# A fused MLP on one core: two sums of each split pair issued one pair later, and the steps of the next input block dealt out anew

## The chip, the core and the metric

The kernel runs on one core of a Trainium2 chip. A core has TensorE (matrix products, with a queue of its own for weight loads, written PEld in the rows), VectorE (DVE), ScalarE (ACT), GpSimd (POOL) and SyncE (SP, which issues transfers here). Each engine works through its own instructions in the order in which the kernel issues them, and waits for others through semaphores. The metric is the device time of one execution in microseconds, as the median of several runs; less is better.

## The reference

Three stages follow each other on 4 x 3072 tokens of 256 channels: a Fourier layer (a transform along the sequence, a complex linear map with soft threshold, the transform back), a channel mix (shift, `relu(xk @ w_k)^2 @ w_v`, gated by a sigmoid), and an MLP with the Mish activation. The change touches the last one alone:

```python
def _moe2_ref(x, w_in, w_out):            # x: 12288 x 256
    h = x @ w_in                          # 256 x 2048
    sp = np.where(h > 20.0, h, np.log1p(np.exp(np.minimum(h, 20.0))))
    g = h * np.tanh(sp)                   # Mish
    return (g @ w_out).astype(np.float32) # 2048 x 256
```

## The kernel before

The MLP takes the tokens in 24 blocks of 512 (`t`, 0 to 23), and each block in eight pairs (`r = P % 8`, of P = 8t + r). A pair is two slices of 128 of the 2048 hidden channels. For every pair TensorE makes the hidden values (`xy` and `z`, two tiles in its accumulation memory), ScalarE takes their Mish, and three pairs later (`LAG = 3`) TensorE multiplies the result by its slice of `w_out` into the block's four output tiles `o`.

Every fp32 operand is split in a high and a low part, and each product is three matmuls: high x high, high x low, low x high. So ScalarE takes each Mish twice, once rounded into `gh` and once in full into `g`, and VectorE makes the low part `gl = g - gh` (line 1137).

From block 1 on, both products of a pair go by a scheme of seven half-size products for eight (Strassen's, in a form with few sums). The first product of all pairs is made in that way (`emit_hS`): sums of the input, `xS`, are made once per block in six steps (`make_xS(t, k)`, k = 0 to 5), for block t+1 during block t, spread over its pairs; steps 0, 1, 3 and 5 stand on VectorE, 2 and 4 on ScalarE. The second product is made in that way for the pairs r = 0, 2, 3, 5, 6 of blocks 1 to 22, called split pairs here (`strassen(P)`, `QS`). A split pair needs four sums of its `g`, made on VectorE into the tile `S6`: two first sums, `sums(P, 0)`, and two second sums, `sums(P, 1)`, of which the last one reads the one before. Then ScalarE rounds the four sums to the high part of `HS` (`high_S`), and VectorE subtracts to get the low part (`low_S`). A split pair's second product is 21 matmuls of 256 columns, that of another pair 12 of 512.

All order is written by hand. `emit_hS(P)` issues a pair in this sequence, with `o(n)` for the next n matmuls of the second product of pair P - 3:

1. TensorE: the first product into `xy`. ScalarE: copy of it to `z` (line 1292), which marks the pair's begin in this document; then `act_1`, the Mish of the last pair's `xy` (in pair 2 of a block first a copy of `o` into the tile `U`, line 1233).
2. `o(n1)`; three products into `xy` and `z`. ScalarE: copy of `xy` to `ub` (line 1298). VectorE: `dve_1`, with the low parts of the last pair and first sums; in pair 2 three sums of `U` (`first_sums`) stand ahead of them, and in pair 0 two transposes of finished output.
3. `o(n2)`; one more product into `xy`, which needs `ub` to be done. VectorE: the addition of `xy` and `ub` into `z`. ScalarE: `act_2`, then the Mish of `z`. VectorE: `dve_2`, with `low_S(P - 2)`, the second sums of pair P - 1 and steps of the next x.
4. The rest of `o`, then two products with `WI` into `xy`, the first of which overwrites what the addition into `z` read. VectorE: the addition of `xy` and `ub` into `xy`. These two products and the first of the next pair are nine matmuls in a row, `xy<-xS,WI x9`.

A tile's buffers are few: `g` has two, `U`, `HS` and `ub` one, so that a pair's `g` is written again two pairs later.

Of the kernel before, what the change touches and what calls it, by code (L numbers as in the profile page):

```python
# [24 lines left out]
NBLK = B * 6  # L25
# [5 lines left out]
def kernel(  # L31
# [27 lines left out]
    nc = tc.nc  # L59
# [10 lines left out]
    def x2_part(c, n):  # L70
        q, o = divmod(c, 1536)
        return x2d[q][:, :, o:o + n]
# [788 lines left out]
    g_t = {}  # L861
# [110 lines left out]
    for t in range(NA + 1):  # L972
# [5 lines left out]
        for i2 in range(4):  # L978
            P = 4 * t + i2
# [68 lines left out]
    def load_x2(t):  # L1048
        v = pb.tile([128, 2, 512], F32, tag="x2", name="x2", bufs=1)
        nc.sync.dma_start(out=v, in_=x2_part(512 * t, 512))  # L1050
        x2_t[t] = v
# [15 lines left out]
    def make_xS(t, k, eng=None):  # L1067

        v = x2_t[t]
        last = t == NBLK - 1  # L1070
        o4 = last_order if last else (lambda a, how=None: a)
        b11, b12, b21, b22 = (
            o4(v[:, j, 256 * h:256 * h + 256], "p (c n w) -> p c w n") for j in range(2) for h in range(2)
        )
        if k == 0:
            xT_t[0] = pb.tile([128, 4, 256], F32, tag="xT", name="xT", bufs=1)
            xS_t[t] = pb.tile([128, 2, 7, 256], F32R, tag="xS", name="xS", bufs=2)
        xT, xS = xT_t[0], xS_t[t]

        def raw(l):  # L1080
            if last:
                return [(o4(xS[:, l, i, :]), b) for i, b in enumerate((b11, b21, b22))]
            return [(xS[:, l, 0, :], b11), (xS[:, l, 1:3, :], v[:, 1, :].rearrange("p (h n) -> p h n", h=2))]

        def xt(o):
            return o4(xT[:, o, :])

        def sub(o, x0, x1):
            nc.vector.tensor_tensor(out=xt(o), in0=x0, in1=x1, op=ALU.subtract)

        def cast(o, x):
            if eng is None:
                nc.vector.tensor_copy(out=o, in_=x)
            else:
                eng.copy(out=o, in_=x)

        if k == 0:
            sub(0, b12, b11)
            sub(2, b22, b12)
        elif k == 1:  # L1100
            sub(1, b22, xt(0))
            sub(3, b21, xt(1))
        elif k == 2:
            cast(xS[:, 0, 3:7, :], xT)
        elif k == 3:
            nc.vector.tensor_tensor(out=xS[:, 1, 3:7, :], in0=xT, in1=xS[:, 0, 3:7, :], op=ALU.subtract)
        elif k == 4:
            for xs, b in raw(0):
                cast(xs, b)
        else:  # L1110
            for (xl, b), (xh, _) in zip(raw(1), raw(0)):
                nc.vector.tensor_tensor(out=xl, in0=b, in1=xh, op=ALU.subtract)
# [9 lines left out]
    def strassen(P):  # L1122
        return 8 <= P < 8 * (NBLK - 1) and P % 8 in QS

    xy_t, low_t, S_t, S_n = {}, {}, {}, []
    S6 = pb.tile([128, 6, 256], F32, name="S6")

    def blocks(v):
        return v.rearrange("p m (h n) -> p (m h) n", h=2)
# [14 lines left out]
    def mish_xy(P):  # L1144
        xy = xy_t.pop(P, None)
        if xy is None:
            return
        ks = (slice(0, 2), slice(1, 3))
        mish(P, xy, (slice(1, 2), slice(2, 3)) if strassen(P) else ks, ks)

    def low(P):
        if low_t.get(P):
            low_t[P].pop(0)()

    def tt(out, x0, x1, op):
        nc.vector.tensor_tensor(out=out, in0=x0, in1=x1, op=op)  # L1156

    def sums(P, k):
        if not strassen(P):
            return  # L1160
        g = blocks(g_t[P][2])
        if k == 0:
            n = len(S_n)
            S_n.append(P)
            S_t[P] = [4 * (n % 2), (0, 2, 1, 3) if n % 2 == 0 else (2, 0, 3, 1)]
            a = S6[:, S_t[P][0]:S_t[P][0] + 2, :]
            tt(a[:, 0, :], g[:, 1, :], g[:, 3, :], ALU.add)
            tt(a[:, 1, :], g[:, 0, :], g[:, 1, :], ALU.subtract)
            return
        a = S_t[P][0]  # L1170
        tt(S6[:, 2, :], S6[:, a, :], g[:, 0, :], ALU.subtract)
        tt(S6[:, 3, :], g[:, 2, :], S6[:, 2, :], ALU.subtract)

# [4 lines left out]
    def high_S(P):  # L1178
        if P in S_t:
            hl = pb.tile([128, 2, 4, 256], F32R, tag="HS", name="HS", bufs=1)  # L1180
            S_t[P].append(hl)
            nc.scalar.copy(out=hl[:, 0], in_=S_of(P))  # L1182

    def low_S(P):
        if P in S_t:
            hl = S_t[P][2]
            tt(hl[:, 1], S_of(P), hl[:, 0], ALU.subtract)
# [6 lines left out]
    def new_U(t):  # L1194
        U_t[t] = pb.tile([128, 4, 256], F32, tag="U", name="U", bufs=1)

    def first_sums(t):
        U, (a, b, c, d) = U_t[t], o_t[t]
        tt(U[:, 3, :], c[:, 1, :], U[:, 0, :], ALU.add)
        tt(U[:, 1:3, :], d, both(U[:, 3, :]), ALU.add)  # L1200
        tt(U[:, 3, :], d[:, 1, :], U[:, 1, :], ALU.add)

    def last_sums(t):
        U = U_t[t]
        for e in range(2):
            o, u = o_t[t][e], U[:, 2 * e:2 * e + 2, :]
            if t:
                tt(u, o, u, ALU.add)
            else:
                nc.vector.tensor_copy(out=u, in_=o)  # L1210

    def put_out(t):
        U = U_t.pop(t)
        ob = pb.tile([128, 16, 32, 2], F32, tag="ob", name="ob", bufs=1)
        for e in range(2):
            nc.vector.transpose(
                out=ob[:, :, :, e], in_=U[:, 2 * e:2 * e + 2, :].rearrange("p h (c w) -> p (h c) w", w=32)
            )
        for m in range(4):
            b, r = divmod(4 * t + m, 24)  # L1220
            j, k = divmod(r, 3)
            dst = out_v[b, j, k].rearrange("n w d -> w n d")
            for i in range(4):
                nc.sync.dma_start(  # L1224
                    out=dst[:, :, 64 * i:64 * i + 64],
                    in_=ob[32 * i:32 * i + 32, 4 * m:4 * m + 4].rearrange("p n d e -> p n (d e)"),
                )

    def act_1(P):
# [3 lines left out]
            nc.scalar.copy(out=U_t[t - 1][:, 0, :], in_=o_t[t - 1][2][:, 0, :])  # L1233
        mish_xy(P - 1)

    def dve_1(P):
        t, r = divmod(P, 8)
        if r == 2 and 1 < t < NBLK:
            first_sums(t - 1)
        if r == 3 and 0 < t < NBLK:  # L1240
            if t == 1:
                new_U(0)
            last_sums(t - 1)
        low(P - 1)
        if t + 1 < NBLK and t:
            if r in (4, 5):
                make_xS(t + 1, 1 if r == 4 else 3)
            if r == 7 and t + 2 < NBLK:
                load_x2(t + 2)
        if r == 7 and t == NBLK - 1:  # L1250
            put_out(t - 1)
        if r == 0 and 1 < t < NBLK:
            put_out(t - 2)
        low(P - 1)
        if r != 3:
            sums(P - 1, 0)

    def act_2(P):
        t, r = divmod(P, 8)
        high_S(P - 2)  # L1260
        if t and t + 1 < NBLK and r in (3, 4):
            make_xS(t + 1, 4 if r == 3 else 2, nc.scalar)

    def dve_2(P):
        t, r = divmod(P, 8)
        low_S(P - 2)
        if r == 3:
            sums(P - 1, 0)
        sums(P - 1, 1)
        if t and t + 1 < NBLK and r in (1, 6):  # L1270
            make_xS(t + 1, 0 if r == 1 else 5)

    def emit_hS(P, o):
        t, r = divmod(P, 8)
# [22 lines left out]
        prod(z[:, 0, :], A(0, 1), 1)  # L1297
        nc.scalar.copy(out=ub, in_=xy)  # L1298
        dve_1(P)
        o(n2)  # L1300
        prod(xy[:, 0, :], S_(0), 3)
        tt(z[:, 1, :], xy[:, 0, :], ub[:, 1, :], ALU.add)
        act_2(P)
        mish_z(P, z)
        dve_2(P)
        o(99)
        prod(xy[:, 0, :], S3, 2)
# [87 lines left out]
    for P in range(2, 8 * NBLK + LAG):  # L1395
        t, q = divmod(P, 8)
        steps = o_steps(P - LAG) if P >= LAG else iter(())

        def o(n):
            for _ in range(n):  # L1400
                if next(steps, 0) == 0:
                    return

        if P < 8 * NBLK:
            if t:
                emit_hS(P, o)
            else:
                emit_h(P)
                if q < 7:
                    make_xS(1, q - 2)  # L1410
                if q == 6:
                    make_xS(1, 5)
                    load_x2(2)
                load_WI(P)
        else:
            act_1(P)
            dve_1(P)
            act_2(P)
            dve_2(P)
        o(99)  # L1420
        t, q = divmod(P - LAG, 8)
        if q in QS and P >= LAG and t in (0, NBLK - 2):
            to_WO(q, b12_d[QS.index(q)] if t else wt_d[QS.index(q)][:, 768:1024])
# [82 lines left out]
```

## Time and profile before

| what | value |
|---|---|
| median of 3 runs | 1926.55 us (1926.35 to 1927.57) |
| the profiled execution, its own time | 1927.98 us |
| its span, from the first to the last instruction | 1926.1 us |
| mean granted clock of TensorE | 0.998 of full speed |
| TensorE busy | 1907.6 us, 99% |
| TensorE weight loads busy | 1823.6 us, 95% |
| VectorE busy | 1403.3 us, 73% |
| ScalarE busy | 1334.2 us, 69% |
| GpSimd busy | 147.2 us, 8% |

The busy time of an engine counts its own instructions, not its waits for semaphores. TensorE's matmuls overlap in their rows and their ends are modelled, so small waits need not show as gaps there; the distance between like points of two pairs shows them. The MLP's pairs with both products fill the span from about 964 us to the end; a block takes some 41 us.

### The profile page before, as it was taken

To read this page: it belongs to the slowest core of one execution; us is meant where nothing else is said; L and a number is where in the kernel's file an instruction comes from. 1 tells how busy PE (TensorE), PEld (TensorE's weight loads), DVE (VectorE), ACT (ScalarE), POOL (GpSimd) and SP (SyncE) were. 2 spreads that over 40 slices of the span, in tenths; PEclk is the share of its full clock that TensorE was granted. 3 is DMA by queue.
4 is the path that set the end of the run, shared out by engine and by line. 5 is a ranking of instruction groups with operands and counts; after the bars stand their busy time and mean duration, and the time that the engine had idled before them with its cause. 6 is when DMAs were issued, how large, how long until landed. Compare 5 with 4: busy or idle time off the path is not lost.

```text
span 1926.1 us, 33928 instructions
## 1 busy us (share of the span) xinstructions
PE 1907.6 (99%) x12964; PEld 1823.6 (95%) x12964; DVE 1403.3 (73%) x2498; ACT 1334.2 (69%) x2315; POOL 147.2 (8%) x236
## 2 busy tenths in 40 slices
PE   8999999999999999999999999999999999999998
PEld 6889989999999999999899999999999999999998
DVE  3788776665665665664378888888888888888884
ACT  4777776666666666666467777777777777777774
POOL 1444630000000000000000000000000000000000
PEclk9999999999999999999999999999999999999999
DMA  9877531322212222220411000111000111000111
GB/s 271 250 235 227 162 112 55 94 73 62 91 50 94 65 66 87 72 75 28 146 40 30 23 23 23 34 28 29 23 23 23 34 27 30 23 23 23 34 25 35
DMA packets 122598, 138.04 MB, mean 72 GB/s; under 512 B 59778, under 2 KB 96100, under 8 KB 122436
## 3 DMA queue, kind: packets, MB, share of 16 engines
q1 hardware_dynamic: 118852, 123.29, 22.4%
q0 software_dynamic: 3584, 12.58, 1.8%
q8 instruction: 102, 1.67, 0.3%
q14 instruction: 60, 0.49, 0.1%
HBM read 78.03 MB, written 57.80 MB: 71 GB/s over the span
## 4 chain that ended last, share of the span: by engine, by line
PE 93%; DVE 2%; POOL 1%; DMA 1%; issue 1%; SPq 1%; ACT 0%; POOLq 0%; DVEq 0%; ACTq 0%
PE o L1355 25%; PE xy L1284 21%; PE kp L755 14%; PE vp L957 14%; PE pp L911 3%; PE z L1284 3%; PE pp L573 3%; PE s1p L361 2%; PE mxp L457 2%; PE s2p L408 1%; PE k1p L457 1%; PE i1p L512 1%; PE hp L877 1%; POOL Y L503 1%; SPq L1224 0%
## 5 line engine op out<-in xcount | busy, mean ns | idle before, releaser
L755 PE MATMUL kp<-xk,WK 128*128 128x384 f32 x1524 | 291.6, 339 | 0.0
L1355 PE MATMUL o<-gh,WO 128*128 128x512 f32 (+1 forms) x1032 | 283.4, 346 | 0.0
L957 PE MATMUL vp<-kh,WV 128*128 128x384 f32 x1024 | 280.7, 335 | 0.0
L944 DVE TENSOR_TENSOR kl<-kr,kh 128x768 fp32r<-128x768 f32 x128 | 122.9, 960 | 211.2 <-ACT kr L943 210.5
L755 PEld LDWEIGHTS kp<-xk,WK 128*128 128x128 f32 x1524 | 264.1, 188 | 0.2
L1284 PE MATMUL xy<-xS,WS 128*128 128x256 f32 x1656 | 261.0, 284 | 0.9 <-ACT z L1292 0.9
L1284 PEld LDWEIGHTS xy<-xS,WS 128*128 128x128 f32 x1656 | 231.0, 189 | 17.9 <-ACT z L1292 1.7
L1137 DVE TENSOR_TENSOR gl<-g,gh 128x512 fp32r<-128x512 f32 x368 | 218.3, 603 | 36.8 <-ACT g L1135 36.8
L1284 PE MATMUL xy<-xS,WI 128*128 128x256 f32 x1656 | 231.0, 284 | 0.0
L1284 PEld LDWEIGHTS xy<-xS,WI 128*128 128x128 f32 x1656 | 211.1, 189 | 9.7 <-DVE z L1156 4.7
L1135 ACT ACTIVATE gh<-z 128x512 fp32r<-128x512 f32 x184 | 110.4, 600 | 145.6 <-PE o L1355 120.3
L957 PEld LDWEIGHTS vp<-kh,WV 128*128 128x128 f32 x1024 | 186.6, 188 | 0.8 <-DVE r L965 0.7
L1355 PEld LDWEIGHTS o<-gh,WO 128*128 128x128 f32 x1032 | 173.7, 188 | 13.9
L1355 PE MATMUL o<-gl,WO 128*128 128x512 f32 (+1 forms) x516 | 178.5, 346 | 0.0
L957 PE MATMUL vp<-kl,WV 128*128 128x384 f32 x512 | 171.5, 335 | 0.0
L942 ACT ACTIVATE kh<-kr 128x768 fp32r<-128x768 f32 x128 | 108.3, 846 | 86.2 <-PE vp L957 85.8
L1156 DVE TENSOR_TENSOR z<-xy,ub 128x256 f32<-128x256 f32 x184 | 79.5, 432 | 94.9 <-PE xy L1284 92.5
L935 ACT ACTIVATE kr<-kp 128x768 f32<-128x768 f32 x127 | 103.3, 813 | 62.5 <-PE kp L755 60.8
L1298 ACT COPY ub<-xy 128x512 f32<-128x512 f32 x184 | 108.4, 589 | 42.1 <-PE xy L1284 41.0
L1156 DVE TENSOR_TENSOR HS<-S,HS 128x1024 fp32r<-128x1024 f32 x110 | 134.2, 1220 | 0.0
L1355 PE MATMUL o<-HS,WO 128*128 128x256 f32 x660 | 131.5, 280 | 0.0
L1182 ACT CAST HS<-S 128x1024 fp32r<-128x1024 f32 x110 | 115.9, 1054 | 2.1 <-PE o L1355 0.3
(177 smaller groups left out, 3846.8 us busy)
## 6 DMA issues: line engine op xcount, KB each, us to landing
scr<-Cs SPq DMA_DIRECT2D x48, 256.0 KB, 2.5
D<-scr SPq DMA_DIRECT2D x32, 384.0 KB, 4.5
x2d<-r POOLq DMA_DIRECT2D x32, 384.0 KB, 2.8
x<-x2d SPq DMA_DIRECT2D x24, 512.0 KB, 3.9
out_dram<-ob SPq DMA_DIRECT2D x368, 32.0 KB, 1.6
A<-scr SPq DMA_DIRECT2D x44, 256.0 KB, 4.4
xs<-in_x_dram SPq DMA_DIRECT2D x24, 384.0 KB, 5.8
scr<-xs SPq DMA_DIRECT2D x24, 384.0 KB, 4.4
```

Of the source, the lines that this page charges most:

```text
L755: nc.tensor.matmul(out=p, lhsT=WK[:, dh, w, f * 128:(f + 1) * 128], rhs=hl[:, v, dh, :], start=(i == 0), stop=(i == 5),)
L935: nc.scalar.activation(out=kr, in_=kp_t.pop(P)[:, :, 0:TA], func=AF.Relu)
L942: nc.scalar.activation(out=kh, in_=kr, func=AF.Square)
L944: nc.vector.tensor_tensor(out=kl, in0=kr, in1=kh, op=ALU.subtract)
L957: nc.tensor.matmul(out=p[:, o, 0:TA], lhsT=WV[:, f, w, o * 128:(o + 1) * 128], rhs=v[:, m, :], start=(f == 0 and i == 0), stop=(f == 7 and ...
L1135: nc.scalar.activation(out=h[:, v[1], :], in_=src[:, v[0], :], func=AF.Mish)
L1137: lambda: nc.vector.tensor_tensor(out=gl[:, hs[1], :], in0=g[:, hs[1], :], in1=gh[:, hs[1], :], op=ALU.subtract)
L1156: nc.vector.tensor_tensor(out=out, in0=x0, in1=x1, op=op)
L1182: nc.scalar.copy(out=hl[:, 0], in_=S_of(P))
L1284: nc.tensor.matmul(out=out, lhsT=a(l), rhs=xS[:, v, b, :], start=(start and n == 0), stop=False, skip_group_check=True)
L1298: nc.scalar.copy(out=ub, in_=xy)
L1355: nc.tensor.matmul(out=out, lhsT=w, rhs=v, start=start, stop=False, skip_group_check=True)
```

## The change

Two things move. The second sums of a split pair stood in `dve_2` of the pair after it; they now stand in `dve_1` of the pair after that, ahead of the low parts (and behind `first_sums` and `last_sums` where these stand). The blocks of `g` that they read are kept in `g_of`. And the steps of the next x, with their pairs r, are set by three tables: step 1 goes from pair 4 to 5, step 3 from 5 to 6 (both in `dve_1`), step 2 from 4 to 5 (`act_2`); steps 4 (pair 3), 0 (pair 1) and 5 (pair 6) keep their pairs. The load of the next x moves from `dve_1` to `dve_2` of pair 7.

```diff
     def sums(P, k):
         if not strassen(P):
             return
-        g = blocks(g_t[P][2])
         if k == 0:
+            g = blocks(g_t[P][2])
             n = len(S_n)
             S_n.append(P)
             S_t[P] = [4 * (n % 2), (0, 2, 1, 3) if n % 2 == 0 else (2, 0, 3, 1)]
+            g_of[P] = g
...
             return
-        a = S_t[P][0]
+        a, g = S_t[P][0], g_of.pop(P)
         tt(S6[:, 2, :], S6[:, a, :], g[:, 0, :], ALU.subtract)
         tt(S6[:, 3, :], g[:, 2, :], S6[:, 2, :], ALU.subtract)
...
+    XS_B = {5: (1,), 6: (3,)}
+    XS_A = {1: (0,), 6: (5,)}
+    XS_C = {3: (4,), 5: (2,)}
+
+    def x_steps(P, table, eng=None):
+        t, r = divmod(P, 8)
+        if t and t + 1 < NBLK:
+            for k in table.get(r, ()):
+                make_xS(t + 1, k, eng)
+
     def dve_1(P):
...
             last_sums(t - 1)
+        if P - 2 in S_t:
+            sums(P - 2, 1)
         low(P - 1)
-        if t + 1 < NBLK and t:
-            if r in (4, 5):
-                make_xS(t + 1, 1 if r == 4 else 3)
-            if r == 7 and t + 2 < NBLK:
-                load_x2(t + 2)
+        x_steps(P, XS_B)
...
     def act_2(P):
-        t, r = divmod(P, 8)
         high_S(P - 2)
-        if t and t + 1 < NBLK and r in (3, 4):
-            make_xS(t + 1, 4 if r == 3 else 2, nc.scalar)
+        x_steps(P, XS_C, nc.scalar)
 
     def dve_2(P):
         t, r = divmod(P, 8)
         low_S(P - 2)
         if r == 3:
             sums(P - 1, 0)
-        sums(P - 1, 1)
-        if t and t + 1 < NBLK and r in (1, 6):
-            make_xS(t + 1, 0 if r == 1 else 5)
+        x_steps(P, XS_A)
+        if r == 7 and 0 < t and t + 2 < NBLK:
+            load_x2(t + 2)
```

The first place is VectorE's row from the addition into `z` of pair 1 to that of pair 2. `S_9457` is the tile `S6`, of which `S<-S,g` is the first and `S<-g,S` the second of the two second sums; `xT` is step 0 of the next x. Before:

```order
L1156 TENSOR_TENSOR z<-xy,ub 128x256
L1156 TENSOR_TENSOR S_9457<-S_9457,g 128x256
L1156 TENSOR_TENSOR S_9457<-g,S_9457 128x256
L1089 TENSOR_TENSOR xT<-x_12711 128x256 x2
L1156 TENSOR_TENSOR xy<-xy,ub 128x256
L1156 TENSOR_TENSOR U<-o_12443,U 128x256
L1156 TENSOR_TENSOR U<-o_12444,U 128x512
L1156 TENSOR_TENSOR U<-o_12444,U 128x256
L1137 TENSOR_TENSOR gl<-g,gh 128x2x256
L1137 TENSOR_TENSOR gl<-g,gh 128x512
L1156 TENSOR_TENSOR z<-xy,ub 128x256
```

The same stretch of VectorE's row after the change:

```order
L1156 TENSOR_TENSOR z<-xy,ub 128x256
L1089 TENSOR_TENSOR xT<-x_12727 128x256 x2
L1156 TENSOR_TENSOR xy<-xy,ub 128x256
L1156 TENSOR_TENSOR U<-o_12443,U 128x256
L1156 TENSOR_TENSOR U<-o_12444,U 128x512
L1156 TENSOR_TENSOR U<-o_12444,U 128x256
L1156 TENSOR_TENSOR S_9457<-S_9457,g 128x256
L1156 TENSOR_TENSOR S_9457<-g,S_9457 128x256
L1137 TENSOR_TENSOR gl<-g,gh 128x2x256
L1137 TENSOR_TENSOR gl<-g,gh 128x512
L1156 TENSOR_TENSOR z<-xy,ub 128x256
```

The two sums of pair 0 have moved from behind `z` of pair 1 to a place between the three sums of `U` and the low parts, ahead of `z` of pair 2.

The second place is VectorE's row from the addition into `z` of pair 7 to that of pair 0 of the next block. `HS` is the low part of the sums of pair 5, and the transposes make finished output. Before:

```order
L1156 TENSOR_TENSOR z<-xy,ub 128x256
L1156 TENSOR_TENSOR HS<-S_9457,HS 128x1024
L1156 TENSOR_TENSOR S_9457<-S_9457,g 128x256
L1156 TENSOR_TENSOR S_9457<-g,S_9457 128x256
L1156 TENSOR_TENSOR xy<-xy,ub 128x256
L1137 TENSOR_TENSOR gl<-g,gh 128x2x256
L1216 STREAM_TRANSPOSE ob<-U 128x512 x2
L1137 TENSOR_TENSOR gl<-g,gh 128x512
L1156 TENSOR_TENSOR z<-xy,ub 128x256
```

After the change:

```order
L1156 TENSOR_TENSOR z<-xy,ub 128x256
L1156 TENSOR_TENSOR HS<-S_9457,HS 128x1024
L1156 TENSOR_TENSOR xy<-xy,ub 128x256
L1156 TENSOR_TENSOR S_9457<-S_9457,g 128x256
L1156 TENSOR_TENSOR S_9457<-g,S_9457 128x256
L1137 TENSOR_TENSOR gl<-g,gh 128x2x256
L1217 STREAM_TRANSPOSE ob<-U 128x512 x2
L1137 TENSOR_TENSOR gl<-g,gh 128x512
L1156 TENSOR_TENSOR z<-xy,ub 128x256
```

Here the addition into `xy` and the two sums of pair 6 have changed places; between the low part of `HS` and `z` of the next pair stand the same instructions.

## Rows read from the trace of the kernel before

**Rows 1.** Windows (stretch, length, busy by engine, granted clock, transfers): pair stage; two early stretches.
```profile
1400.00:1600.00 200.00, 199.98 (x1504) 190.70 (x1503) 170.45 (x342) 146.20 (x278) 0.00 (x0) 1.00 0.11 27
52.00:54.00 2.00, 1.07 (x9) 1.11 (x10) 0.79 (x2) 0.40 (x1) 0.00 (x0) 1.00 1.06 213
...
8.00:16.00 8.00, 7.80 (x20) 5.08 (x21) 1.37 (x2) 1.16 (x2) 0.00 (x0) 0.57 1.02 273
```

**Rows 2.** Waits from 965 us on: who waited for whom, us, times, longest.
```profile
DVE U L1156 <- ACT U L1233: 8.0, 21, 0.7
PEld xy L1284 <- DVE z L1156: 4.7, 22, 0.5
```

**Rows 3.** Timeline of ScalarE, block 10: start, us, instruction, idle before.
```profile
1334.57 0.36 ACT L1292 COPY z<-xy 128x256 f32<-128x256 f32 x1 [0.25 <-PE xy L1284]
1335.46 0.60 ACT L1135 ACTIVATE gh<-xy 128x512 fp32r<-128x512 f32 x1 [0.53 <-DVE xy L1156]
...
1336.43 0.59 ACT L1298 COPY ub<-xy 128x512 f32<-128x512 f32 x1
...
1339.71 0.36 ACT L1292 COPY z<-xy 128x256 f32<-128x256 f32 x1 [0.18 <-PE xy L1284]
...
1344.73 0.36 ACT L1292 COPY z<-xy 128x256 f32<-128x256 f32 x1 [0.20 <-PE xy L1284]
1345.00 0.38 ACT L1233 COPY U<-o 128x256 f32<-128x256 f32 x1
...
1350.04 0.36 ACT L1292 COPY z<-xy 128x256 f32<-128x256 f32 x1 [0.29 <-PE xy L1284]
...
1360.34 0.36 ACT L1292 COPY z<-xy 128x256 f32<-128x256 f32 x1 [0.18 <-PE xy L1284]
1361.21 0.60 ACT L1135 ACTIVATE gh<-xy 128x512 fp32r<-128x512 f32 x1 [0.51 <-DVE xy L1156]
...
1365.47 0.36 ACT L1292 COPY z<-xy 128x256 f32<-128x256 f32 x1 [0.18 <-PE xy L1284]
```

**Rows 4.** Timeline of VectorE, the same block.
```profile
1335.00 0.43 DVE L1156 TENSOR_TENSOR xy<-xy,ub 128x256 f32<-128x256 f32 x1
...
1337.80 0.43 DVE L1156 TENSOR_TENSOR z<-xy,ub 128x256 f32<-128x256 f32 x1
...
1343.14 0.41 DVE L1156 TENSOR_TENSOR S<-S,g 128x256 f32<-128x256 f32 x1
1343.59 0.43 DVE L1156 TENSOR_TENSOR S<-g,S 128x256 f32<-128x256 f32 x1
1343.93 0.75 DVE L1089 TENSOR_TENSOR xT<-x 128x256 f32<-128x256 f32 x2
...
1345.41 1.61 DVE L1156 TENSOR_TENSOR U<-o,U 128x256 f32<-128x256 f32 x3 [0.38 <-ACT U L1233]
1346.94 1.28 DVE L1137 TENSOR_TENSOR gl<-g,gh 128x512 fp32r<-128x512 f32 x2
1348.14 0.42 DVE L1156 TENSOR_TENSOR z<-xy,ub 128x256 f32<-128x256 f32 x1
...
1349.63 0.43 DVE L1156 TENSOR_TENSOR xy<-xy,ub 128x256 f32<-128x256 f32 x1
...
1361.68 1.22 DVE L1106 TENSOR_TENSOR xS<-xT,xS 128x1024 fp32r<-128x1024 f32 x1
...
1368.58 0.43 DVE L1156 TENSOR_TENSOR z<-xy,ub 128x256 f32<-128x256 f32 x1 [0.83 <-PE xy L1284]
...
1375.38 0.43 DVE L1156 TENSOR_TENSOR S<-S,g 128x256 f32<-128x256 f32 x1
```

**Rows 5.** Timeline of TensorE: the nine matmuls at the end of pairs 2 and 7.
```profile
1348.69 1.26 PE L1284 MATMUL xy<-xS,WI 128*128 128x256 f32 x9
...
1374.45 1.24 PE L1284 MATMUL xy<-xS,WI 128*128 128x256 f32 x9
```

**Rows 6.** Timeline of the weight loads: those of the nine matmuls of pair 2.
```profile
1348.62 1.12 PEld L1284 LDWEIGHTS xy<-xS,WI 128*128 128x128 f32 x9 [0.20 <-DVE z L1156]
```

More of the change, by code (lines that the diff above doesn't have):

```diff
@@ L1123, in strassen @@
         return 8 <= P < 8 * (NBLK - 1) and P % 8 in QS
-    xy_t, low_t, S_t, S_n = {}, {}, {}, []
+    xy_t, low_t, S_t, S_n, g_of = {}, {}, {}, [], {}
     S6 = pb.tile([128, 6, 256], F32, name="S6")
```

## The prediction

> **What bounds the kernel now.** I read the windows of the pair stage first, then the chain of waits, then the lines of ScalarE, VectorE and TensorE through one block of eight pairs. Pair r of a block is counted from its copy of xy to z on ScalarE. Over 200 us of the stage TensorE is busy for 199.98 us at a granted clock of 1.00 [rows 1], while VectorE has 170 us of work: the stage ends when TensorE ends, and VectorE counts only where TensorE waits for it. So I looked for places where TensorE is late although its row shows no gap, by comparing pairs with the same matmuls. Pairs 0, 1 and 5 each issue 42 matmuls of 256 columns; from one z copy to the next they take 5.14, 5.02 and 5.13 us [rows 3]. Pair 2 (12 matmuls of 512 columns in place of 21) takes 5.31 us.
>
> Why pairs 0 and 5 lose 0.11 to 0.12 us: ScalarE's Mish of the old xy waits 0.53 us (pair 0) and 0.51 us (pair 5) for VectorE's last addition into xy [rows 3]. In pair 0 that addition starts at 1335.00 us [rows 4], 0.43 us into the pair, because the two second sums of the pair before stand ahead of it. The Mish pushes ub back to 1336.43 us, and TensorE's product behind ub starts late.
>
> Pair 2 is the other tight place. VectorE finishes xy of pair 1, then waits 0.38 us for ScalarE's copy of U, and from 1345.41 us runs without a gap: three sums of U, two low parts, z at 1348.14 us [rows 4]. The weight load of the next product waits for that z [rows 6], and its matmul follows at 1348.69 us [rows 5]. Both waits recur: 21 for U, 22 for z [rows 2].
>
> **The change, part by part.** No instruction is added or removed, they are dealt out anew.
>
> *The second sums move from behind z in pair P+1 to the front of pair P+2.* The two instructions are 0.45 us apart, the second one waiting for the first, and the next starts 0.34 us after the second [rows 4]: a place in the row costs 0.79 us. They move in five pairs of each block; the place decides.
>
> - Into pair 2 (sums of pair 0). As the order shows, they stand behind the three U sums, which wait for ScalarE's U copy; the 0.79 us that pair 1 gives up in front of that wait only makes VectorE idle longer there. From U to z there is no idle time in which to put them, so z goes from 1348.14 to 1348.93 us and the product from 1348.69 to 1349.48 us. Queued behind the sums on VectorE are the two low parts and z; TensorE waits for z and has used up its other matmuls of the pair. Of the 0.79 us TensorE can absorb at most the 0.20 us for which only the weight load waited [rows 6]: the ends are 0.59 us and 0.88 us (the sums' two durations, 0.41 and 0.43, and the 0.04 us between them). I take 0.79, since z to matmul is a chain with no idle time. It holds in blocks 2 to 22: block 1 has no U sums there and block 23 no second sums. 21 x 0.79 = 16.6 us; ends 12.4 and 18.5.
> - Out of pair 4 (into 5). The xy addition of pair 4 no longer follows the sums, so the Mish in pair 5 need not wait 0.51 us. Pair 5 falls to the length of pair 1: 0.11 us x 22 = 2.4 us gained; ends 0 and 2.6.
> - Out of pair 7 (into 0). Here I expect far less. Before, the sums start at 1375.38 us [rows 4], xy 0.79 us later and the low part 0.34 us after that, at 1376.51. After, xy comes first, but it needs its own product: in pair 2 it started 0.94 us after the nine matmuls of WI began (1349.63 against 1348.69), so here 1374.45 + 0.94 = 1375.39 us [rows 4, 5]; the sums and the low part follow, 0.34 + 0.45 + 0.34 later, at 1376.52. VectorE reaches the low part when it did before. From xy to z it runs without a gap in pair 0 (transposes of the output stand there; z at 1337.80 carries no idle time [rows 4]), so z stays nearly where it is: ub is early, but z is late next. I put 0.03 us x 22 = 0.7 us on it; ends 0 and 22 x 0.12 = 2.6.
> - Into pairs 4 and 7 they take the time that they leave in the pair before; VectorE's z there waits for TensorE. Nothing.
>
> VectorE: DVE Perf Modes, a page of the Trainium skill, says in "The DRAIN you can't avoid" that a semaphore between two instructions costs nothing beyond the flush that every instruction has. The rows differ: 0.45 us behind a dependent sum, 0.34 us otherwise. By the page the two would cost 0.68 us, the term of pair 2 would be 14.3 us and the total 2.3 us less.
>
> *Steps of the next x.* Step 1 goes from pair 4 to 5, step 3 from 5 to 6, the cast of step 2 on ScalarE from 4 to 5. Step 3 lasts 1.22 us; in pair 6 it meets VectorE idle for 0.83 us before z [rows 4] and, before that, waiting for ScalarE's g, so nothing; if only the 0.83 us covered it, 0.39 x 22 = 8.6 us. Pair 5 loses step 3 and gains step 1 and the sums, but begins 0.8 us earlier on VectorE: nothing. The cast lands on ScalarE behind the cast of HS, as it did in pair 4; pair 4 has wide matmuls as pair 2 has, so pair 5 will be about 0.29 us shorter (5.31 against 5.02), and ScalarE then waited 0.18 us at the end of pair 4 (the z copy at 1360.34 us [rows 3]), so the next z copy could be 0.11 us late. TensorE has seven matmuls before it needs that copy: nothing, at most 0.11 x 22 = 2.4 us.
>
> *The load of the next x* is issued on SyncE behind the same readers, one half-pair later in program order, with no other transfer between, and is first read in the second pair after: nothing. The g buffers are read longer, by a sum at the head of the pair that writes them again behind z, on ScalarE: z comes later than the sum, nothing.
>
> Sum: 16.6 - 2.4 - 0.7 = **+13.5 us**. The profiled execution has a span of 1926.1 us and took 1927.98 us, so it would take 1941.5; it lies 1.43 us over the median of 1926.55 us. From the median: **1940.0 us**, 0.70% slower.
>
> **The rivals.**
>
> *Faster: the wait for U swallows the sums.* If U's copy is not what holds the first U sum, but the late xy of pair 1, the U sums start 0.79 us earlier and the sums fill the hole: pair 2 keeps its length, and the gain of 3.1 us (5.2 with both gains at their ends) stays: 1923.4, at best 1921.3. For it speaks that xy of pair 1 ends only 0.38 us before U. Against it: the wait is for ScalarE's U, 21 times [rows 2], and the copy, at 1345.00 us for 0.38 us, ends 0.03 us before U starts. It decides if that copy could come 0.6 us earlier, and it stands directly behind the z copy, which waits for TensorE [rows 3].
>
> *TensorE absorbs part.* If the 0.20 us of the weight load are slack and both gains come at their ends: 12.4 - 5.2 = 7.2 us, 1933.8.
>
> *The new waits cost TensorE its clock.* Each block then has a wait of about 0.8 us more. In the rows TensorE idles for almost half of a 2 us stretch (1.07 us busy) and keeps a granted clock of 1.00; only the start shows less, 0.57 in a stretch that TensorE worked 7.80 of 8 us [rows 1], so part of it at the lower level. Should each wait throw the clock to 1.2 GHz of 2.4 for a pair, a pair of 5.02 us would take up to 5.02 us more: 21 x 5.0 = 105 us, 2045. The Trainium skill, TensorE: Matmul & The Clock Gate, "A second HAM failure mode: psum-queue depth-cycling", reports such a swing where TensorE idles briefly and often between groups of matmuls; by that rule this rival would hold. The 1.00 of the idle stretch speaks against it.
>
> **How the numbers follow.** Forecast (pair 2 pays 0.6 to 0.9 us, small gains elsewhere) 0.86; TensorE absorbs part, 0.05; the wait for U swallows the sums, 0.07; the clock, 0.02. The forecast's bounds are 12.4 - 5.2 = +7 and 18.5 - 0.2 = +18; 1934 to 1944 us holds most of it and of the second case, over 8 in 10. Against 0.2% (3.9 us, about what a measurement of this kernel can tell from no change): the U rival lies across that border with 3.1 to 5.2 us, so 0.04 of it counts as the same and 0.03 as faster; slower 0.93.
>
> **What would show it.** Right: in blocks 2 to 22 pair 2 takes about 6.1 us, the weight load there waits about 1 us for z (some 20 us over 21 times, against 4.7 us in 22), VectorE's idle time before U grows from 0.38 to about 1.1 us, pair 5 takes 5.02 us and its Mish of xy no longer waits for VectorE, pair 0 stays above 5.08. Wrong: pair 2 under 5.6 us; or pairs 0 and 5 both at 5.02 us (then the gain of pair 0 was mis-sized); or a granted clock under 0.99 in the stage.

## The result and the profile after

The changed kernel takes 1946.5 us (median of 4 runs, 1945.71 to 1947.54) against 1926.45 us before (4 runs, 1925.72 to 1927.57). The ratio is 1.0095, with a 95% interval of 1.0083 to 1.0107: slower by 16 to 21 us. The forecast was slower by 13.5 us, 1940.0 us, with a range up to 1944: the sign held, the size did not.

A pair's length is the time from its z copy on ScalarE to the next one. Medians over the 22 or 23 blocks, in us, and the sum of all pairs against before (the later kernels are those of the experiments):

| kernel | 0 | 1 | 2 | 3 | 4 | 5 | 6 | 7 | stage against before |
|---|---|---|---|---|---|---|---|---|---|
| before | 5.14 | 5.02 | 5.31 | 5.01 | 5.28 | 5.14 | 5.01 | 5.28 | |
| changed | 5.03 | 5.02 | 6.10 | 5.01 | 5.27 | 5.34 | 4.99 | 5.28 | +17.5 |
| e1_front | 5.02 | 5.02 | 5.35 | 5.01 | 5.29 | 5.34 | 4.98 | 5.28 | +2.5 |
| e2_cast | 5.03 | 5.02 | 6.11 | 5.01 | 5.28 | 5.01 | 5.02 | 5.27 | +12.1 |
| e3_both | 5.03 | 5.01 | 5.35 | 5.02 | 5.29 | 5.01 | 5.03 | 5.26 | -4.7 |
| e4_tables | 5.14 | 5.01 | 5.31 | 5.02 | 5.28 | 5.35 | 4.97 | 5.28 | +4.0 |
| e5_hs2 | 5.03 | 5.02 | 6.10 | 5.02 | 5.27 | 5.01 | 5.01 | 5.27 | +11.3 |
| e6_least | 5.03 | 5.02 | 5.31 | 5.02 | 5.28 | 5.01 | 5.03 | 5.27 | -4.6 |

Of the +17.5 us, pair 2 brings +16.3, pair 5 +4.5, pair 0 -2.3, pair 6 -0.7, the rest -0.2. The span grew by 19.6 us; another 2.2 us of that lie ahead of the stage, which begins at 965.8 us in place of 963.6. All eight kernels have the same work up to there, and their profiles reach it between 961.8 and 966.2 us, so I count those 2 us as a difference between executions, not as the change.

The profiles point to the granted clock of the first 60 us. Each has a stretch there at the lower of its two levels, 1.2 of 2.4 GHz. The profile before has it from 8.9 to 15.7 us, that of the changed kernel from 38.2 to 45.1 us. The windows from 39 to 45 us, before and after (columns as in the next fence):

```profile
39.00:45.00 6.00, 6.00 (x49) 5.74 (x48) 4.10 (x8) 3.09 (x5) 0.75 (x2) 1.00 0.70 222
...
39.00:45.00 6.00, 6.00 (x22) 4.91 (x22) 3.12 (x6) 1.02 (x2) 0.00 (x0) 0.50 0.71 239
```

The three kernels with a low stretch at 38 to 46 us reach the pair stage at 965.5 to 966.2 us, the other five by 964.2. No run varies this clock alone, so that it makes the 2 us is not shown. But e5_hs2, whose profile has its low stretch early, begins the stage at 963.7 us with the order of the changed kernel.

The windows of the pair stage (stretch, length, then busy time of TensorE, weight loads, VectorE, ScalarE, GpSimd, granted clock, transfers) answer to [rows 1]:

```profile
1400.00:1600.00 200.00, 197.20 (x1473) 187.08 (x1474) 168.58 (x339) 143.77 (x272) 0.00 (x0) 1.00 0.10 25
```

TensorE now stands still for 2.8 us of 200, at the same clock of 1.00.

The waits of the changed kernel, answering to [rows 2] (who waited for whom, us, times, longest). The edit moves its line numbers: the z copy is line 1299, the copy of U 1234, the cast of HS 1183; the first product is on line 1291, the second on 1362.

```profile
PEld xy L1291 <- DVE z L1156: 21.1, 22, 1.0
ACT HS L1183 <- DVE S L1156: 18.7, 21, 0.9
ACT HS L1183 <- PE o L1362: 14.9, 43, 0.3
DVE U L1156 <- ACT U L1234: 14.5, 22, 0.7
PE xy L1291 <- DVE z L1156: 11.9, 21, 0.6
...
PEld xy L1291 <- ACT z L1299: 6.9, 26, 1.4
```

The weight loads' wait for z grew from 4.7 to 21.1 us, and TensorE itself now shows a wait in 21 blocks. The second row is new: the cast of HS waits for the second sums. Before, the third and the last row stood at 0.3 us each: ScalarE now waits for TensorE before it rounds HS, and weight loads wait for ScalarE's z copy.

VectorE in pairs 0 to 2 of block 10 (start, us, instruction, idle before), against [rows 4]:

```profile
1343.18 0.43 DVE L1156 TENSOR_TENSOR xy<-xy,ub 128x256 f32<-128x256 f32 x1
...
1344.32 0.68 DVE L1137 TENSOR_TENSOR gl<-g,gh 128x512 fp32r<-128x512 f32 x1
1344.92 1.30 DVE L1217 STREAM_TRANSPOSE ob<-U 128x512 f32<-128x512 f32 x2
1346.14 0.65 DVE L1137 TENSOR_TENSOR gl<-g,gh 128x512 fp32r<-128x512 f32 x1
1346.71 0.43 DVE L1156 TENSOR_TENSOR z<-xy,ub 128x256 f32<-128x256 f32 x1
...
1353.22 0.43 DVE L1156 TENSOR_TENSOR xy<-xy,ub 128x256 f32<-128x256 f32 x1 [0.42 <-PE xy L1291]
1354.31 1.61 DVE L1156 TENSOR_TENSOR U<-o,U 128x256 f32<-128x256 f32 x3 [0.66 <-ACT U L1234]
1355.83 0.42 DVE L1156 TENSOR_TENSOR S<-S,g 128x256 f32<-128x256 f32 x1
1356.28 0.42 DVE L1156 TENSOR_TENSOR S<-g,S 128x256 f32<-128x256 f32 x1
1356.63 1.28 DVE L1137 TENSOR_TENSOR gl<-g,gh 128x512 fp32r<-128x512 f32 x2
1357.83 0.43 DVE L1156 TENSOR_TENSOR z<-xy,ub 128x256 f32<-128x256 f32 x1
```

In pair 2, from U to z, VectorE takes 3.52 us (1354.31 to 1357.83), before 2.73: the two sums cost 0.79 us there, and VectorE idles longer ahead of U, 0.66 us in place of 0.38. The time that the sums free in pair 1 comes back as idle time: 0.42 us for TensorE ahead of xy and 0.28 us more ahead of U. TensorE's row shows the same delay, in answer to [rows 5]:

```profile
1357.35 0.39 PE L1362 MATMUL o<-gl,WO 128*128 128x512 f32 x1
1358.31 1.33 PE L1291 MATMUL xy<-xS,WI 128*128 128x256 f32 x9 [0.57 <-DVE z L1156]
```

The late sums hold up ScalarE's cast of HS in pair 2 as well, by 0.9 us. That is not what TensorE waits for: behind the cast ScalarE itself stands idle for 0.56 us until z is there:

```profile
1356.74 1.05 ACT L1183 CAST HS<-S 128x1024 fp32r<-128x1024 f32 x1 [0.90 <-DVE S L1156]
1358.35 0.60 ACT L1135 ACTIVATE gh<-z 128x512 fp32r<-128x512 f32 x1 [0.56 <-DVE z L1156]
```

ScalarE in pairs 5 and 6 of the same block, against [rows 3]:

```profile
1370.02 0.36 ACT L1299 COPY z<-xy 128x256 f32<-128x256 f32 x1 [0.25 <-PE xy L1291]
1370.29 0.61 ACT L1135 ACTIVATE gh<-xy 128x512 fp32r<-128x512 f32 x1
...
1371.56 0.59 ACT L1305 COPY ub<-xy 128x512 f32<-128x512 f32 x1 [0.18 <-PE xy L1291]
1372.50 1.05 ACT L1183 CAST HS<-S 128x1024 fp32r<-128x1024 f32 x1 [0.35 <-PE o L1362]
1373.45 1.05 ACT L1095 CAST xS<-xT 128x1024 fp32r<-128x1024 f32 x1
1374.40 0.59 ACT L1135 ACTIVATE gh<-z 128x512 fp32r<-128x512 f32 x1
1374.89 0.59 ACT L1135 ACTIVATE g<-z 128x512 f32<-128x512 f32 x1
1375.36 0.39 ACT L1299 COPY z<-xy 128x256 f32<-128x256 f32 x1
```

The Mish of xy no longer waits for VectorE (0.51 us before), and ub comes early. But then the cast of HS waits 0.35 us for TensorE, the cast of step 2 follows without a gap, and ScalarE is busy up to the next z copy, which it makes 5.34 us after the last. The weight loads of the next pair that need that copy come late:

```profile
1375.37 0.19 PEld L1362 LDWEIGHTS o<-HS,WO 128*128 128x128 f32 x1
1375.80 0.77 PEld L1291 LDWEIGHTS xy<-xS,WS 128*128 128x128 f32 x6 [0.24 <-ACT z L1299]
```

### The profile page after: what moved, and what is told of

It is laid out like the page before. It is cut to its first block, busy times and chain, and to the rows that moved or that the text cites. A ratio compares the mean times of both kernels' runs of the same rounds, so it can differ in the third digit from the quotient of the medians.

```text
span 1945.7 us, 33882 instructions
## 1 busy us (share of the span) xinstructions
PE 1912.0 (98%) x12964; PEld 1822.7 (94%) x12964; DVE 1408.0 (72%) x2498; ACT 1331.8 (68%) x2315; POOL 146.9 (8%) x236
## 3 DMA queue, kind: packets, MB, share of 16 engines
q1 hardware_dynamic: 118852, 123.29, 22.2%
## 4 chain that ended last, share of the span: by engine, by line
PE 88%; DVE 5%; issue 2%; DMA 2%; POOL 1%; ACT 1%; SPq 0%; ACTq 0%; POOLq 0%
PE o L1362 21%; PE xy L1291 20%; PE kp L755 14%; PE vp L957 14%; PE pp L911 3%; PE z L1291 3%; PE pp L573 3%; PE mxp L457 2%; PE s1p L361 2%; DVE U L1156 2%; PE s2p L408 1%; PE k1p L457 1%; PE i1p L512 1%; DMA XS<-in_x_dram 1%; DVE gl L1137 1%
## 5 line engine op out<-in xcount | busy, mean ns | idle before, releaser
L1291 PEld LDWEIGHTS xy<-xS,WI 128*128 128x128 f32 x1656 | 210.9, 189 | 26.2 <-DVE z L1156 21.1
```

The costliest lines, as they stand in the source:

```text
L1291: nc.tensor.matmul(out=out, lhsT=a(l), rhs=xS[:, v, b, :], start=(start and n == 0), stop=False, skip_group_check=True)
```

## The experiments

The theory after the result: two separate losses, the sums of pair 0 behind U (pair 2), and the cast of step 2 behind a late cast of HS (pair 5), less the gain of the moved sums in pairs 0 and 5. Each difference below is against the changed kernel, except where it says otherwise. Ratios are against the kernel before on the same chip.

**e1_front: the sums of pair 0 ahead of the sums of U.**

```diff
     def dve_1(P):
+        if r == 2 and P - 2 in S_t:
+            sums(P - 2, 1)
         if r == 2 and 1 < t < NBLK:
             first_sums(t - 1)
...
-        if P - 2 in S_t:
+        if r != 2 and P - 2 in S_t:
             sums(P - 2, 1)
```

> The changed kernel with one difference: in pair 2 of a block the two second sums of pair 0 stand ahead of the three sums of U, in the time for which VectorE waits for ScalarE's copy of U. Theory (it is their place behind that wait that costs 0.79 us in each of 21 blocks): pair 2 falls from 6.10 to about 5.35 us, the other pairs stay; 1946.5 - 16 = about 1930.5 us. Rival (the sums cost wherever they stand in the row of pair 2, since VectorE has no room there): pair 2 stays near 6.1 us, the time near 1946.5.

Measured: 1930.69 us, ratio 1.0011 (1.0002 to 1.0020); pair 2 takes 5.35 us. VectorE at the head of pair 2:

```profile
1345.99 0.43 DVE L1156 TENSOR_TENSOR xy<-xy,ub 128x256 f32<-128x256 f32 x1 [0.42 <-PE xy L1293]
1346.33 0.42 DVE L1156 TENSOR_TENSOR S<-S,g 128x256 f32<-128x256 f32 x1
1346.78 0.43 DVE L1156 TENSOR_TENSOR S<-g,S 128x256 f32<-128x256 f32 x1
1347.12 1.60 DVE L1156 TENSOR_TENSOR U<-o,U 128x256 f32<-128x256 f32 x3
```

The sums now fill the time that VectorE had spent waiting for U, and U starts without an idle tag, 0.04 us later in the pair than before (0.72 us after the z copy at 1346.40, against 0.68). The same five instructions in another order are worth 0.75 us a block. It was the place behind the wait that cost, not the sums.

**e2_cast: steps 1 and 2 of the next x back in pair 4.**

```diff
-    XS_B = {5: (1,), 6: (3,)}
+    XS_B = {4: (1,), 6: (3,)}
...
-    XS_C = {3: (4,), 5: (2,)}
+    XS_C = {3: (4,), 4: (2,)}
```

> The changed kernel with steps 1 and 2 of the next x back in pair 4 (step 3 stays in pair 6, the sums stay moved). Theory (ScalarE is late at the end of pair 5 because the cast of step 2 stands behind a cast of HS that itself starts only when the single HS buffer is free): pair 5 falls from 5.34 to about 5.02 us, pair 6 rises from 4.99 to 5.01; 22 blocks x 0.3 = 6.5 us less, about 1940. Rival (the sums at the head of VectorE's row in pair 5 hold it up): pair 5 stays at 5.3 us and the time near 1946.5.

Measured: 1940.3 us, ratio 1.0061 (1.0045 to 1.0076); pair 5 takes 5.01, pair 6 5.02 us. The sums still stand at the head of VectorE's row in pair 5, so they are not what made it long. Step 1 went back together with the cast, so this run does not tell those two apart. But e5_hs2 keeps both in pair 5, which takes 5.01 us there: step 1 does no harm in it, and the row that is busy up to the next z copy is ScalarE's, with the cast. In pair 4 the same two casts follow each other, and the next z copy waits for TensorE as it did before:

```profile
1361.96 0.36 ACT L1299 COPY z<-xy 128x256 f32<-128x256 f32 x1 [0.30 <-PE xy L1291]
...
1364.09 1.06 ACT L1183 CAST HS<-S 128x1024 fp32r<-128x1024 f32 x1
1365.04 1.05 ACT L1095 CAST xS<-xT 128x1024 fp32r<-128x1024 f32 x1
...
1367.25 0.36 ACT L1299 COPY z<-xy 128x256 f32<-128x256 f32 x1 [0.18 <-PE xy L1291]
...
1369.72 1.05 ACT L1183 CAST HS<-S 128x1024 fp32r<-128x1024 f32 x1 [0.35 <-PE o L1362]
```

In pair 4 the cast of HS starts with no wait, 2.13 us into the pair; in pair 5 it waits 0.35 us for TensorE here too, but nothing stands behind it that is short of time.

**e3_both: both of these.** The edits of e1_front and e2_cast together.

> Both of these at once: sums of pair 0 ahead of the sums of U, steps 1 and 2 in pair 4. Theory: pair 2 about 5.35, pair 5 and pair 0 about 5.02 us, so the gain of the moved sums stays and the two losses go: 1946.5 - 16 - 6.5 = about 1924, some 2 to 4 us under the kernel before. Rival (one of the two only moves its wait elsewhere): 1927 or more.

Measured: 1923.43 us, ratio 0.9976 (0.9967 to 0.9985), 2.9 to 6.4 us under the kernel before. The two losses are separate: in the stage the first edit alone takes off 15.0 us (17.5 - 2.5), the second 5.4, both 22.2. That is 1.8 more than their sum; 1.1 us of it lie in pairs 1 and 4 of e1_front, which are 0.4 and 0.7 us longer in all than before and as before in e3_both.

**e4_tables: the steps of the next x as changed, the second sums where they stood before.**

```diff
     def dve_1(P):
...
-        if P - 2 in S_t:
-            sums(P - 2, 1)
...
     def dve_2(P):
...
+        sums(P - 1, 1)
         x_steps(P, XS_A)
```

> Only the steps of the next x as in the changed kernel; the second sums stand where they stood before. Theory (the cast of step 2 alone makes pair 5 long): pair 2 stays at 5.31, pair 0 at 5.14, pair 5 goes from 5.14 to about 5.34 us: 22 x 0.2 = 4.4 us more than before, about 1931. Rival (pair 5 is long because of the sums): no difference from before, 1926.5.

Measured: 1932.12 us, ratio 1.0024 (1.0014 to 1.0034); pairs 0 and 2 stay at 5.14 and 5.31, pair 5 takes 5.35 us. The new tables alone lose 4.0 us in the stage. With the sums in their old place ScalarE's Mish of xy waits for VectorE again, and still pair 5 is as long as in the changed kernel: its end is set by ScalarE's row from the cast of HS on, and the gain that the sums would bring there is covered by it.

**e5_hs2: two buffers for the high part of HS.**

```diff
-            hl = pb.tile([128, 2, 4, 256], F32R, tag="HS", name="HS", bufs=1)
+            hl = [pb.tile([128, 4, 256], F32R, tag=n, name=n, bufs=b) for n, b in (("HSh", 2), ("HSl", 1))]
             S_t[P].append(hl)
-            nc.scalar.copy(out=hl[:, 0], in_=S_of(P))
+            nc.scalar.copy(out=hl[0], in_=S_of(P))
...
-            rhs = raw[v][:, x, :] if x >= 0 else hl[:, v, pos[-1 - x], :]
+            rhs = raw[v][:, x, :] if x >= 0 else hl[v][:, pos[-1 - x], :]
```

> The changed kernel with the high part of HS in a tile of its own with two buffers (the low part keeps one); all order as in the changed kernel. Theory (in pair 5 ScalarE's cast of HS starts 0.35 us late because TensorE still reads the single buffer, and this pushes the cast of step 2, the Mish of z and the next z copy): the cast of HS starts about 2.05 us into pair 5 in place of 2.48, pair 5 falls from 5.34 to about 5.03 us, 22 x 0.3 = 6.6 us less than the changed kernel, about 1940; pair 2 stays at 6.10. Rival (two casts of 1.05 us are too much for ScalarE in a pair of narrow matmuls, whatever the buffer): pair 5 stays at 5.25 us or more, the time at 1944 or more.

Measured: 1938.9 us, ratio 1.0051 (1.0037 to 1.0064); pair 5 takes 5.01, pair 2 6.10 us. ScalarE in pair 5, with the order of the changed kernel:

```profile
1365.25 0.36 ACT L1299 COPY z<-xy 128x256 f32<-128x256 f32 x1 [0.25 <-PE xy L1291]
...
1366.79 0.59 ACT L1305 COPY ub<-xy 128x512 f32<-128x512 f32 x1 [0.18 <-PE xy L1291]
1367.28 1.06 ACT L1183 CAST HSh<-S 128x1024 fp32r<-128x1024 f32 x1
1368.22 1.05 ACT L1095 CAST xS<-xT 128x1024 fp32r<-128x1024 f32 x1
...
1370.26 0.36 ACT L1299 COPY z<-xy 128x256 f32<-128x256 f32 x1
```

The cast of HS starts 2.03 us into the pair in place of 2.48, and the next z copy comes after 5.01 us. Two casts in a pair of narrow matmuls (256 columns) just fit; what made them not fit is the single buffer, which TensorE still reads. The edit also parts the high from the low part, so the run does not say whether that alone would do.

**e6_least: the sums of pair 0 stay in pair 1, the others move; steps 1 and 2 in pair 4.** The tables of e2_cast, and:

```diff
     def dve_1(P):
...
-        if P - 2 in S_t:
+        if r != 2 and P - 2 in S_t:
             sums(P - 2, 1)
...
     def dve_2(P):
...
+        if r == 1:
+            sums(P - 1, 1)
         x_steps(P, XS_A)
```

> The second sums moved in all pairs but one: those of pair 0 stay in pair 1, behind z, as before the change; steps 1 and 2 of the next x in pair 4, step 3 in pair 6. Theory (moving the sums of pair 0 gains nothing anywhere, all the gain comes from pairs 0 and 5, where the Mish of xy no longer waits for VectorE): pair 2 5.31, pairs 0 and 5 about 5.02 us; 5 us under before, about 1922 to 1923, within 1 us of the kernel with the sums ahead of U. Rival (the move of pair 0's sums has a gain of its own, in pair 1): pair 1 longer than 5.02 and the time 2 us or more over that kernel's.

Measured: 1924.18 us, ratio 0.9973 (0.9962 to 0.9985). Pair 1 stays at 5.02 and pair 2 at 5.31 us: moving the sums of pair 0 gains nothing. This kernel and e3_both can't be told apart (their intervals overlap almost wholly); both beat the kernel before.

## Why the prediction was wrong in its size

*Pair 2: right.* I forecast 16.6 us in blocks 2 to 22 from a chain without idle time; it is 16.3, at the place and through the wait named, and e1_front takes it away by the order alone. VectorE's idle time ahead of U grew to 0.66 us only, not to 1.1: the other 0.42 us came as a wait ahead of xy. The row of the changed kernel has the two sums 0.45 us apart and the next instruction 0.35 us later, 0.80 in all. The Trainium skill says that a semaphore after each instruction costs nothing extra (VectorE: DVE Perf Modes, "The DRAIN you can't avoid"). The trace does not agree: by that pair 2 would have grown by 0.68 us, and it grew by 0.79.

*The cast of step 2: wrong, the step that failed.* I wrote that it lands behind the cast of HS "as it did in pair 4", that the next z copy could be 0.11 us late, and that TensorE had cover: nothing, at most 2.4 us. It cost 7.3 us in pair 5, which is 5.34 us long, and 5.01 with the cast in pair 4 or with a second buffer (22 x 0.33); pair 6 gives back 0.8 of it. So the copy was late by 0.33 us, and the seven matmuls covered some 0.04 us of that. What I missed is that the cast of HS does not start behind ub in pair 5 as it does in pair 4. TensorE reads HS in a pair whose partner three pairs back is split: pair 5 (partner 2) does, and is still reading the only buffer; pair 4 (partner 1) does not. From the cast of HS to the next z copy ScalarE has 2.86 us of work without a gap (1372.50 to 1375.36); begun 2.13 us into the pair, as in pair 4, it would end at 4.99 us, but begun at 2.48 it ends at 5.34. In the kernel before this wait was there and did not show, as its ScalarE rows in pair 5 tell. The last line below, a weight load, is the one that needs the z copy of pair 6: that copy, of 0.36 us from 1365.47 [rows 3], ended only 0.11 us ahead of it.

```profile
1362.18 0.59 ACT L1298 COPY ub<-xy 128x512 f32<-128x512 f32 x1
1362.83 1.06 ACT L1182 CAST HS<-S 128x1024 fp32r<-128x1024 f32 x1
...
1365.94 0.78 PEld L1284 LDWEIGHTS xy<-xS,WS 128*128 128x128 f32 x6
```

The cast started 2.49 us after that pair's z copy [rows 3], against 2.48 in the changed kernel: the same time, but behind a late ub, with only 0.06 us of idle time left. The early ub that the moved sums bring made the wait show in the row; it is not what made the pair long, for in e4_tables ub is late as before and pair 5 takes 5.35 us.

*Pair 5: the gain did not come, for that reason.* Forecast -2.4 us by the sums, measured +4.5 us with the cast; the two together explain it, since with the cast back the pair gains 2.8 us (e2_cast, e3_both).

*Pair 0: right in sign, mis-sized.* Forecast -0.7 us, measured -2.3. I took VectorE to be the limit from xy to z because z carried no idle tag. The rows show that it was not: before, the low part started at 1337.15 us, lasted 0.65 and z started at its very end, 1337.80; after, the low part at 1346.14 lasts 0.65 and z starts at 1346.71, 0.08 us before its end, as other neighbours on VectorE do. So z before had been waiting for TensorE in the shadow of the low part: a reading of the rows, which no run tests by itself. The line of before:

```profile
1337.15 0.65 DVE L1137 TENSOR_TENSOR gl<-g,gh 128x512 fp32r<-128x512 f32 x1
```

The other half of that step held: the first low part starts 0.73 us into the pair against 0.76.

*Pair 6* lost nothing to step 3, as forecast, and is 0.03 us shorter because it begins late: with step 3 still there it takes 5.01 us in e5_hs2.

*The rivals.* The wait for U did not swallow the sums: VectorE waits 14.5 us for it, 22 times. TensorE absorbed nothing. Its clock stayed at 1.00 with a wait of about 0.57 us in each of 21 blocks [rows 1, and the window of the pair stage above]. The Trainium skill (TensorE: Matmul & The Clock Gate, "A second HAM failure mode: psum-queue depth-cycling") reports a swinging clock where TensorE idles briefly and often between groups of matmuls; that did not show here, at one such wait in some 41 us.

*The sum and the range.* From the forecast of +13.5 us to the stage's +17.5, pair 5 brings 6.9 us, pair 0 -1.6, pair 2 -0.3, pair 6 -0.7 and the rest -0.2. The stage alone would have made about 1944 us, the very end of the range; that the time lies beyond it is owed to the 2 us ahead of the stage as well. The range was also too narrow by my own terms: its upper end, 18.5 - 0.2, holds nothing of the 2.4 us that I gave as the most the cast could cost.

What the runs leave open are those 2 us. In e1_front to e4_tables and in e6_least the time against before agrees with the stage against before to 0.2 us; in e5_hs2 it is 1.3 us less, in the changed kernel 2.5 us more. That speaks for scatter between executions, but no run times that part by itself.

## What to carry to other kernels

Price an instruction where it lands, not where it leaves: on an engine that keeps its order, moved work is cheap where it comes to stand ahead of a wait, and costs in full behind the wait where no idle time follows (here 0.04 against 0.79 us). Before you call a place like another one ("as it did in pair 4"), look up for the neighbours of the moved instruction which buffers they write and who still reads these; a wait that another delay covers has no row, and comes out when you remove the delay. And look at start and end of back-to-back instructions: where the second one usually starts before the first one's end and here does not, it waits, idle tag or not.

## What the runs showed of the hardware

VectorE starts an independent instruction 0.34 us after an addition of 128x256 fp32 that lasts 0.42, so the two overlap by 0.08 us; an addition that reads the other's result starts 0.45 us after it. A matmul stage in which TensorE waits 0.57 us in every 41 us or so kept a granted clock of 1.00 (mean of the window from 1400 to 1600 us).
